# Second chunk of v loaded earlier and transposed by DMA instead of by TensorE, in a fused attention and gated-FFN kernel

## Chip, cores, metric

One core of one Trainium2 chip. The metric is the device time of one execution in microseconds (us), median of several runs. Lower is better.

## The reference

```python
qn = q / (norm(q, axis=1) + 1e-06)          # q, k, v: [4, 6016, 256] float32
kn = k / (norm(k, axis=1) + 1e-06)
a  = softmax(kn.transpose(0, 2, 1) @ qn / tau)       # [4, 256, 256]
x  = (v @ a).reshape(24064, 256)
gate = sigmoid(x @ w_gate); val = x @ w_val          # d_ff 1536
out  = (gate * val) @ w_out
```

## The kernel before

The kernel folds the softmaxed 256 x 256 matrix into the weights (G = a @ w_gate, H = a @ w_val), so the FFN reads v itself. It works through four batches of v in chunks of 512 rows, 12 chunks a batch. A chunk has 12 steps of 128 FFN columns, each with two matmuls for `ps_gate`, two for `ps_val`, a sigmoid on ScalarE and a product on VectorE. The output matmuls of a chunk run in the steps of the next one.

The FFN needs v transposed. For all chunks but the first two this is a transposing DMA on SP's queue. All loads but two (the first chunk of q and of k, at the very start) convert float32 to bf16 and go through GpSimd's queue.

```python
    def transpose_v(b, ci, ps=None, late=None):
        t0, nt = groups[ci]
        v_sb = vs.pop((b, ci))
        vT = vtpool.tile([P, TPC * CB, P], BF16, tag="vT", name="vT")
        flat = v_sb[:, :nt, :].rearrange("p t c -> p (t c)")
        if ps is None:
            nc.sync.dma_start_transpose(out=vT[:, : nt * CB, :], in_=flat)
        else:
            for n in range(nt * CB):
                nc.tensor.transpose(out=ps[:, n, :], in_=flat[:, ds(n * P, P)], identity=ident_bf)
            half = nt * CB // 2
            nc.vector.tensor_copy(out=vT[:, :half, :], in_=ps[:, :half, :])
            (nc.scalar.copy if late is None else late)(vT[:, half : nt * CB, :], ps[:, half : nt * CB, :])
        ...
    # loads, after q and k of batch 0 and chunk 0 of v
    for fg in range(NFG):                       # three groups of 512 columns
        for w, src in enumerate((moe_w_gate, moe_w_val)):
            nc.gpsimd.dma_start(out=w_sb[w][fg], in_=...)
    load_v(0, 1)
    nc.gpsimd.dma_start(out=w_out_sb, in_=...)
    ...
    # side work of batch b, by slot = chunk * 12 + step
            if (nb, nci) == (0, 1):
                at(7, lambda: transpose_v(0, 1, psm.tile(...)))      # TensorE
            elif nb < B:
                at(ci * FC + 2, transpose_v, nb, nci)                # DMA
            if lb < B:
                at(ci * FC + 0, load_v, lb, lci)
        ...
            at(max(0, s0 - 20), load_qk, n, t0, nt)                  # next batch
```

A slot only fixes the order of instructions within each queue. GpSimd and SP run ahead of TensorE as far as their own waits let them.

## Time and profile before

| | before |
|---|---|
| time, median of the 3 first runs | 831.2 us (830.94 to 831.29) |
| span of the profiled run | 829.0 us |
| TensorE busy | 816.1 us, 98% of the span |
| TensorE idle after 37 us | one wait of 0.36 us, at 51.95 |
| DMA engines | 9 tenths busy or more up to some 80 us, less after |

The lines that carry this are in the prediction. In a timeline row, the first two numbers are start and length, and the bracket at the end tells how long the engine sat idle before it and what released it. TensorE is the bound, so only what TensorE does or waits for counts.

### The profile page before, as it was taken

How to read it: one execution, taken by the hardware profiler on the slowest of the kernel's cores; microseconds unless marked ns; L12 is line 12 of the kernel's file. 1: busy time of each engine (PE TensorE's matmuls, PEld its weight loads, DVE VectorE, ACT ScalarE, POOL GpSimd, SP SyncE). 2: the span in 40 equal slices, each digit the busy share in tenths (PEclk: the TensorE clock that was granted, in tenths of full speed). 3: DMA queues.
4: the chain of work that ended last, by engine and by line, in shares of the span. 5: the costliest groups of instructions: out<-in, count | busy, mean ns of one | idle time of the engine just before them, and what ended most of it. 6: DMA issues, size and time to landing. Idle time of an engine off the chain costs nothing.

```text
span 829.0 us, 13765 instructions
## 1 busy us (share of the span) xinstructions
PE 816.1 (98%) x5192; PEld 502.6 (61%) x5206; DVE 588.9 (71%) x1022; ACT 391.6 (47%) x644; POOL 83.1 (10%) x159
## 2 busy tenths in 40 slices
PE   7899999999999999999999999999999999999998
PEld 4556666665665666665575666666566566666666
DVE  6577777887667777778767777777766666666664
ACT  4654444446644444445654444444655444444442
POOL 5531100002120100000211010000000000000000
PEclk9999999999999999999999999999999999999999
DMA  9999623226946433223875352223323423322111
GB/s 209 207 206 207 113 52 86 57 60 131 159 87 124 96 85 60 57 52 84 156 140 126 81 105 59 51 63 75 64 62 63 72 52 87 67 48 73 43 36 71
DMA packets 78739, 77.17 MB, mean 93 GB/s; under 512 B 50769, under 2 KB 55633, under 8 KB 78673
## 3 DMA queue, kind: packets, MB, share of 16 engines
q0 software_dynamic: 23920, 38.81, 28.3%
q1 hardware_dynamic: 54608, 36.97, 17.6%
q8 instruction: 40, 0.66, 0.3%
q10 hardware_dynamic: 144, 0.52, 0.2%
q14 instruction: 27, 0.21, 0.1%
HBM read 78.64 MB, written 24.64 MB: 125 GB/s over the span
## 4 chain that ended last, share of the span: by engine, by line
PE 94%; DMA 4%; DVE 1%; issue 0%; POOL 0%; ACT 0%; POOLq 0%; ACTq 0%
PE ps_o L88 30%; PE ps_gate L88 29%; PE ps_val L88 29%; PE ps_s L88 4%; DMA q_sb<-in_q_dram 3%; PE ps_gh L88 2%; DMA w_val<-in_moe_w_val_dram 1%; DVE hT L423 0%; ACT g_sb L422 0%; DVE sq L176 0%; PE ps_n L88 0%; POOL k_sb L97 0%; POOL q_sb L97 0%; PE ps_tp L393 0%; DVE out_sb L449 0%
## 5 line engine op out<-in xcount | busy, mean ns | idle before, releaser
L423 DVE TENSOR_TENSOR hT<-ps_val,g_sb 128x512 bf16<-128x512 f32 (+1 forms) x576 | 391.2, 680 | 206.3 <-ACT g_sb L422 201.9
L422 ACT ACTIVATE g_sb<-ps_gate 128x512 bf16<-128x512 f32 (+1 forms) x576 | 338.1, 588 | 386.0 <-PE ps_gate L88 380.0
L88 PE MATMUL ps_gate<-vT,gh_G 128*128 128x512 bf16 (+1 forms) x1152 | 337.6, 375 | 0.6 <-ACT g_sb L422 0.4
L88 PE MATMUL ps_val<-vT,gh_H 128*128 128x512 bf16 (+1 forms) x1152 | 337.4, 375 | 0.4
L88 PE MATMUL ps_o<-w_out_sb,hT 128*128 128x256 bf16 x2256 | 326.2, 273 | 0.0
L88 PEld LDWEIGHTS <-hT 128*128 128x128 bf16 x2256 | 220.7, 98 | 124.8
L88 PEld LDWEIGHTS <-gh_H 128*128 128x128 bf16 x1152 | 112.7, 98 | 131.6 <-issue 1.4
L88 PEld LDWEIGHTS <-gh_G 128*128 128x128 bf16 x1152 | 112.4, 98 | 38.5 <-issue 0.6
L106 POOL DMA_DIRECT2D v_sb<-in_v_dram x48 | 25.6, 533 | 619.9 <-DMA vT<-v_sb 485.8
L449 DVE COPY out_sb<-ps_o 128x256 f32<-128x256 f32 x188 | 77.9, 414 | 13.5 <-PE ps_o L88 13.5
L88 PE MATMUL ps_s<-k_sb,q_sb 128*128 128x256 bf16 x376 | 66.0, 272 | 5.7 <-DMA k_sb<-in_k_dram 4.3
L88 PEld LDWEIGHTS <-q_sb 128*128 128x128 bf16 x376 | 36.6, 98 | 14.1 <-issue 6.3
L215 DVE TENSOR_TENSOR acc<-acc,sq 128x1024 bf16<-128x1024 bf16 (+1 forms) x66 | 44.2, 669 | 0.0
L176 DVE TENSOR_TENSOR sq<-q_sb 128x1024 bf16<-128x1024 bf16 (+2 forms) x44 | 29.4, 668 | 2.7 <-DMA q_sb<-in_q_dram 2.7
L97 POOL DMA_DIRECT2D k_sb<-in_k_dram x48 | 26.3, 549 | 16.5 <-DMA k_sb<-in_k_dram 8.9
L97 POOL DMA_DIRECT2D q_sb<-in_q_dram x48 | 26.2, 545 | 16.0 <-DMA q_sb<-in_q_dram 8.6
L176 DVE TENSOR_TENSOR sq<-k_sb 128x1024 bf16<-128x1024 bf16 (+2 forms) x34 | 22.4, 658 | 0.9 <-ACT sq L174 0.9
L376 ACT ACTIVATE gh_G<-ps_gh,rrow 128x512 bf16<-128x512 f32 x21 | 14.4, 687 | 12.7 <-PE ps_gh L88 8.8
L174 ACT ACTIVATE sq<-k_sb 128x1024 bf16<-128x1024 bf16 (+1 forms) x11 | 11.2, 1018 | 14.6 <-DMA k_sb<-in_k_dram 11.8
L88 PE MATMUL ps_busy<-ones_wide,ones_bf 128*128 128x512 bf16 x57 | 16.3, 412 | 1.7 <-DVE shift L127 1.6
L378 DVE TENSOR_SCALAR gh_H<-ps_gh,rrow 128x512 bf16<-128x512 f32 x22 | 16.4, 743 | 1.6 <-PE ps_gh L88 1.6
L472 DVE TENSOR_TENSOR acc<-acc,sq 128x1024 bf16<-128x1024 bf16 x16 | 11.1, 692 | 5.1 <-ACT sq L174 4.8
(65 smaller groups left out, 124.5 us busy)
## 6 DMA issues: line engine op xcount, KB each, us to landing
out_dram<-out_sb SPq DMA_DIRECT2D x44, 512.0 KB, 2.9
v_sb<-in_v_dram POOLq DMA_DIRECT2D x44, 256.0 KB, 3.8
q_sb<-in_q_dram POOLq DMA_DIRECT2D x43, 256.0 KB, 7.8
k_sb<-in_k_dram POOLq DMA_DIRECT2D x43, 256.0 KB, 8.5
out_dram<-out_sb SPq DMA_DIRECT2D x4, 384.0 KB, 2.5
w_gate<-in_moe_w_gate_dram POOLq DMA_DIRECT2D x3, 256.0 KB, 6.8
w_val<-in_moe_w_val_dram POOLq DMA_DIRECT2D x3, 256.0 KB, 7.4
w_out_sb<-in_moe_w_out_dram POOLq DMA_DIRECT2D x1, 768.0 KB, 12.6
```

Source lines behind the costliest of these rows:

```text
L88: nc.tensor.matmul(out, lhsT=lhsT, rhs=rhs, start=start, stop=stop, **kw)
L97: nc.gpsimd.dma_start(out=tl[:, :nt, :], in_=rows(src, b)[:, t0 : t0 + nt, :])
L106: nc.gpsimd.dma_start(out=v_sb[:, :nt, :], in_=rows(v, b)[:, t0 : t0 + nt, :])
L174: nc.scalar.activation(out=sq[:, :nt, :], in_=src[:, :nt, :], func=ACT.Square)
L176: engine.tensor_tensor(out=sq[:, :nt, :], in0=src[:, :nt, :], in1=src[:, :nt, :], op=ALU.mult)
L215: nc.vector.tensor_tensor(out=acc[:, :nt, :], in0=acc[:, :nt, :], in1=st[b]["sq", w][:, :nt, :], op=ALU.add)
L376: nc.scalar.activation(out=dst, in_=ps, func=ACT.Copy, scale=r)
L378: nc.vector.tensor_scalar(out=dst, in0=ps, scalar1=r, scalar2=None, op0=ALU.mult)
L422: nc.scalar.activation(out=g_sb[:, :n], in_=ps_gate[:, :n], func=ACT.Sigmoid)
L423: nc.vector.tensor_tensor(out=hts[b, ci][:, f, :n], in0=ps_val[:, :n], in1=g_sb[:, :n], op=ALU.mult)
L449: nc.vector.tensor_copy(out=out_sb[:, s, :], in_=ps)
L472: nc.vector.tensor_tensor(out=acc[w], in0=acc[w], in1=sq[w], op=ALU.add)
```

## The change

It takes TensorE's eight transposes and the two copies that follow them out of the first chunk. So that the transposing DMA which replaces them can start in time, v's second chunk is loaded one place earlier.

```diff
     for fg in range(NFG):
+        if fg == NFG - 1:
+            load_v(0, 1)
         for w, src in enumerate((moe_w_gate, moe_w_val)):
             nc.gpsimd.dma_start(...)
-    load_v(0, 1)
     nc.gpsimd.dma_start(out=w_out_sb, ...)
@@
-            if (nb, nci) == (0, 1):
-                at(7, lambda: transpose_v(0, 1, psm.tile(...)))
-            elif nb < B:
-                at(ci * FC + 2, transpose_v, nb, nci)
+            if nb < B:
+                at(ci * FC + (0 if (b, ci) == (0, 0) else 2), transpose_v, nb, nci)
```

More of the change, by code (lines that the diff above doesn't have):

```diff
@@ L526, in side_work @@
             lb, lci = (b, ci + 2) if ci + 2 < NCH else (b + 1, ci + 2 - NCH)
-            if (nb, nci) == (0, 1):
-                at(7, lambda: transpose_v(0, 1, psm.tile([P, TPC * CB, P], BF16, tag="m", name="ps_tp")))
-            elif nb < B:
-                at(ci * FC + 2, transpose_v, nb, nci)
+            if nb < B:
+                at(ci * FC + (0 if (b, ci) == (0, 0) else 2), transpose_v, nb, nci)
             if lb < B:
```

## The prediction

> **What bounds the kernel now.** I read the page's first part and its chain first, then TensorE's timeline around the one spot that the diff touches, then the same stretch of the chain, then the tile of the transposed v, and last the DMA queues in three windows.
>
> The page:
>
> ```profile
> PE 816.1 (98%) x5192; PEld 502.6 (61%) x5206; DVE 588.9 (71%) x1022; ACT 391.6 (47%) x644; POOL 83.1 (10%) x159
> ...
> PE 94%; DMA 4%; DVE 1%; issue 0%; POOL 0%; ACT 0%; POOLq 0%; ACTq 0%
> ```
>
> TensorE is busy for 98% of the span and is 94% of the chain that ended last. From 37 us, when the first weight matrix lands, the chain is nearly all matmuls in program order. So whatever leaves TensorE's order, or whatever gap closes in it, moves the end by as much, and a new gap does the opposite.
>
> TensorE's timeline, 47.95 to 53.97 us (start, length, engine, operation, count, idle before). The removed work lies here: v's second chunk goes through TensorE at step 7 of 12 of the first chunk.
>
> ```profile
> 48.39 0.59 PE L88 MATMUL ps_gate<-vT,gh_G 128*128 128x512 bf16 x2
> 48.82 0.59 PE L88 MATMUL ps_val<-vT,gh_H 128*128 128x512 bf16 x2
> 49.25 0.61 PE L393 MATMUL ps_tp<-ident_bf,v_sb 128*128 128x128 bf16 x8
> 49.70 0.59 PE L88 MATMUL ps_gate<-vT,gh_G 128*128 128x512 bf16 x2
> ...
> 50.56 0.59 PE L88 MATMUL ps_gate<-vT,gh_G 128*128 128x512 bf16 x2
> ...
> 51.95 0.59 PE L88 MATMUL ps_gate<-vT,gh_G 128*128 128x512 bf16 x2 [0.36 <-ACT g_sb L422]
> 52.67 0.59 PE L88 MATMUL ps_val<-vT,gh_H 128*128 128x512 bf16 x2
> 53.10 0.59 PE L88 MATMUL ps_gate<-vT,gh_G 128*128 128x512 bf16 x2
> ...
> 53.97 0.59 PE L88 MATMUL ps_gate<-vT,gh_G 128*128 128x512 bf16 x2
> ```
>
> A step without extras takes 0.86 us (49.70 to 50.56). The step with the transposes takes 1.31 (48.39 to 49.70), two later ones 1.39 and 1.15. The row at 53.97 is the first matmul of chunk 1, the first reader of the tile that the change makes differently.
>
> The chain of waits over the same stretch says why two later steps are long:
>
> ```profile
> 50.72 0.45 PE ps_gate L88 x2
> ...
> 51.30 0.61 ACT g_sb L422
> ...
> 51.93 0.70 DVE hT L423
> ...
> 52.67 0.59 PE ps_val L88 x2
> ```
>
> ScalarE copied half of the transposed tile at 50.81 for 0.59 us, after VectorE had copied the other half. That pushed its next sigmoid to 51.30, VectorE's product to 51.93, and TensorE's next ps_val, which waits for that PSUM buffer, to 52.67.
>
> The transposed tile (first window 48 to 50 us, second 124 to 126): its DMA form lands very differently in the two.
>
> ```profile
> L390 SPq DMA_TRANSPOSE vT<-v_sb x1: 1337/1337/1337, 49.0 to 49.0; - x1
> ...
> DMA to landing us min/median/max: 16.2/16.2/16.2
> ```
>
> ```profile
> DMA to landing us min/median/max: 3.7/3.7/3.7
> ```
>
> The DMA queues while the 16.2 us one moved its data (52.8 to 64.5 us):
>
> ```profile
> q0 software_dynamic: 1083, 1.99, 94.8%
> q1 hardware_dynamic: 1054, 0.26, 17.8%
> ```
>
> and while the output weights came in (42.8 to 46.4 us):
>
> ```profile
> q0 software_dynamic: 1356, 0.72, 144.6%
> ```
>
> The loads (q0) leave no room: the page's DMA row is at 9 tenths for the first tenth of the span. The transpose (q1) moves 256 KB in about 1,024 packets of 256 B and gets just about one packet for each of q0's.
>
> **What the Trainium skill says.** "DMA: Bandwidth & Descriptors", section "Queues, rings and completion order": an engine takes turns between the queues it has work for, one packet each. The trace agrees: 1,083 packets of q0 beside 1,054 of q1. "Advanced Engine Details and Errata", section "X-Bar Transpose (TRN2)": "TRN2 transpose DMAs are as fast as regular DMAs". In the quiet part this holds (3.7 us, against the 3.8 us of the page's median v load of as many bytes); in the saturated part it doesn't, 16.2 us against 12.6 for the v load just before it. "TensorE: Matmul & The Clock Gate", section "Part 4: PE-mode transpose": the result goes to PSUM and has to be copied out, some 275 ns for one in a kernel. The copies are what cost here; the matmul record is 219 ns, and eight pipelined ones advance TensorE by 0.45 us.
>
> **The change part by part.**
>
> 1. Removed from TensorE: eight transposes, 49.25 to 49.70, 0.45 us.
> 2. Removed from ScalarE and VectorE: copies of 0.59 and 0.41 us. On TensorE they cost the two long steps: 1.39 - 0.86 = 0.53, and 1.15 - 0.86 = 0.29. Without them each step gives ScalarE 0.59 and VectorE 0.68 us of work in 0.86, so I expect no wait to replace them. Sum of 1 and 2: about 1.25 us. Check: 48.39 to 53.97 is 5.58 us for five steps; five at 0.865 are 4.33. Chunk 1 could start at 52.7.
> 3. Moved: the load of chunk 1 of v takes the place of the third gate weights in q0. They landed at 41.2 us (issued 33.18, 8.0 later), the value weights at 42.5 (33.87 + 8.6), v at 43.7 (34.58 + 9.1). All are 256 KB, 1.26 us each at the 208 GB/s of this stretch. So v lands at about 41.1 and the weights at 42.4 and 43.7. TensorE reads these first at 44.07 and 45.37, so both keep about 1.6 us. No cost.
> 4. Added: one DMA transpose on SP. The program puts it in step 0, but SP waits only for v and has nothing ahead of it: issue at about 41.15. The existing one, issued at 48.97, showed its first packet at 52.85, 3.9 us later; in the quiet part it was 1.7. If the extra 2.2 us is a fixed number of q0's packets ahead of it, the smaller packets here (1 KB, then 512 B, where the other had 2 KB) halve it: first packet between 43.8 and 45.0.
>    Then the sharing. While the other transpose ran, q0 moved 1.99 MB in 11.7 us, 170 GB/s; without it q0 moves 208. It lost 0.45 MB, 2.1 us of its time, so one transpose packet takes 2.1 x 16 / 1,054 = 32 ns of an engine. It got 88 packets per us (1,024 in the 11.65 us from first to last). The output weights alone: 1,356 packets in 3.6 us, 377 per us, 42 ns a packet on each engine, and they would end at about 46.6. Beside such small ones a pair takes 42 + 32 = 74 ns, so 216 pairs per us.
>    Start at 43.8: all 1,024 run beside the output weights in 4.7 us and end at 48.5. The other one landed 0.7 us after its last packet, so this one at 49.2. Start at 45.0: 377 x 1.6 = 603 pairs in 2.8 us, the other 421 beside 2 KB loads at 88 per us in 4.8, end 52.6, landed at 53.3. Needed at 52.7. By the same sum the break-even start is 44.8.
> 5. Given back by the queue: q0 loses 2.1 us to the new transpose. The output weights land at 49.8 instead of 47.7 (issued 35.11, 12.6 to landing), needed at 54.83 - 1.25 = 53.6. The next batch's first k (issued 39.11, 12.3) lands at 53.5, needed at 57.87 - 1.25 = 56.6. Chunk 2 of v lands near 51.0 instead of 48.9; its transpose then lands at 51.0 + 16.2 = 67.2, needed at 70.88 - 1.25 = 69.6. In time, by 2.4 us where it was 5.7.
>
> Sum: -1.25 us if the transpose is in time: 831.2 - 1.25 = 829.95, call it 830.0.
>
> **The rivals.**
>
> A. The transpose comes late and TensorE waits at the start of chunk 1, a new gap in place of the old ones. For: 16.2 us for its sibling, taken over whole, would land at 57.4; the gap is 4.7 us and the time 831.2 + 3.4 = 834.6. Against: small packets on the other queue through most of it. The late case of step 4, landing at 53.3, waits 0.6 and leaves -0.65: 830.5.
>
> B. The gain stays but the second transpose, now pushed back, is late for chunk 2. For: margin shrinks, and a first packet held up behind the first transpose, then still under way, would shrink it more. Each us late costs one: perhaps 831 to 832.
>
> C. The ScalarE and VectorE copies were hiding another wait, so only the 0.45 us comes back: 830.7. Against: both engines have slack of 0.18 us or more in a plain step.
>
> D. Late weights. It needs over 1.6 us of error in a landing; 832 at most.
>
> **Range and chances.** I give about 60% to on time (829.8 to 830.2), 25% to a partly filled gap or C (830.3 to 831.2), 15% to A or B beyond break-even, up to 834.6. Predicted 830.2 us, 8 in 10 within 829.6 to 832.4. A change of 2% is 16.6 us, and nothing here reaches a third of that either way: faster 0.5%, same 99%, slower 0.5%.
>
> **What would show it right or wrong.** Right: no ps_tp rows after 37 us; steps 7 to 11 of chunk 0 at 0.86 us each; chunk 1's first ps_gate near 52.7 with no idle before it; the new transpose issued near 41.1 and landed before 52.7, so in under 11.6 us; the weights of the third group in before 44.1 and 45.4; the second transpose landed before 69.6. Wrong: an idle of TensorE before chunk 1's first ps_gate released by the DMA of the transposed tile (A), the same at chunk 2 (B), waits on g_sb left in steps 9 to 11 (C), or on w_gate or w_val in steps 3 and 4 (D). A first packet later than 44.8, or a transpose packet dearer than 32 ns, is the likeliest error.

## The result

| | before | changed |
|---|---|---|
| time, median of 6 runs | 831.21 us (830.94 to 831.69) | 834.25 us (832.10 to 836.04) |
| span of the profiled run | 829.0 | 833.3 |

The ratio is 1.0035, 95% interval 1.0018 to 1.0051. Ratios here are the mean time of one kernel's runs over that of the other's in the same rounds, so not quite the ratio of the medians. The changed kernel is slower by 3 us, and its runs spread over 4 us where those of before spread over 0.75.

The page of the changed kernel, its engine line and its chain:

```profile
PE 816.1 (98%) x5184; PEld 502.0 (60%) x5198; DVE 588.5 (71%) x1021; ACT 391.2 (47%) x643; POOL 83.4 (10%) x159
...
PE 90%; DMA 8%; DVE 1%; POOL 0%; issue 0%; ACT 0%; POOLq 0%
```

The eight matmuls are gone from TensorE (5,184 for 5,192), and the DMA's share of the chain went from 4% to 8%. That share alone decides nothing: the last but two of the runs below (`e11_hold_lead8`), as fast as the kernel before, has 8% too. TensorE's timeline of the changed kernel:

```profile
49.37 0.59 PE L88 MATMUL ps_gate<-vT,gh_G 128*128 128x512 bf16 x2
...
51.97 0.59 PE L88 MATMUL ps_gate<-vT,gh_G 128*128 128x512 bf16 x2
...
55.27 0.60 PE L88 MATMUL ps_gate<-vT,gh_G 128*128 128x512 bf16 x2 [2.27 <-DMA vT<-v_sb]
...
91.86 0.61 PE L88 MATMUL ps_gate<-vT,gh_G 128*128 128x512 bf16 x2 [2.38 <-DMA vT<-v_sb]
```

49.37 to 51.97 is three steps of 0.87 us: the steps are as short as forecast. Then TensorE waits twice on the transposed tile: at 55.27 for chunk 1, whose transpose the change added, and at 91.86 for chunk 3, whose transpose was there before and was in time then.

The sum closes: TensorE's first step of chunk 1 could have begun at 51.97 + 0.87 = 52.84 and began at 55.27, where the kernel before began it at 53.97, so +1.30. From the first to the second store of results the delay against before grows from 1.31 to 3.86 us, so chunk 3 adds 2.55. The two stores in SP's timeline, changed:

```profile
74.50 0.34 SPq L452 DMA_DIRECT2D out_dram<-out_sb  x1
...
94.18 0.33 SPq L452 DMA_DIRECT2D out_dram<-out_sb  x1
```

and before:

```profile
73.19 0.35 SPq L451 DMA_DIRECT2D out_dram<-out_sb  x1
...
90.32 0.34 SPq L451 DMA_DIRECT2D out_dram<-out_sb  x1
```

The delay then stays at 3.8 to 3.9 up to the last stores, and about 0.5 us more lies after them: 4.3, the difference of the two spans.

How long the transposes took. First the tile's landing times in the changed kernel, chunk 1's and chunk 3's, then chunk 3's in the kernel before:

```profile
DMA to landing us min/median/max: 13.9/13.9/13.9
...
DMA to landing us min/median/max: 16.8/16.8/16.8
```

```profile
DMA to landing us min/median/max: 10.6/10.6/10.6
```

The queues of the changed kernel, from the issue of chunk 1's transpose to its first packet (41.3 to 45.3 us), while it ran (45.3 to 54.7), and while chunk 3's ran (79.9 to 91.3):

```profile
q0 software_dynamic: 1350, 0.80, 138.7%
...
q0 software_dynamic: 1134, 1.49, 94.8%
q1 hardware_dynamic: 1053, 0.26, 25.3%
...
q0 software_dynamic: 707, 1.27, 67.3%
q1 hardware_dynamic: 1081, 0.33, 21.2%
```

and of the kernel before while chunk 3's ran (79.3 to 83.9):

```profile
q1 hardware_dynamic: 1055, 0.26, 64.2%
q0 software_dynamic: 233, 0.41, 48.5%
```

For 4 us after its issue chunk 1's transpose moves nothing, then it shares packet for packet with the loads (1,134 beside 1,053) for 9.4 us. Chunk 3's transpose met 233 packets of loads in the kernel before and meets 707 in the changed one.

Why it meets more, from GpSimd's timeline. GpSimd's transfers wait for one another: in these rows none is issued before the one eight places ahead of it has landed (48.02 after the output weights at 47.7, and 52.84 after 52.5 in the changed kernel). The load of chunk 3 of v stands eight places behind the output weights. Before:

```profile
48.02 0.53 POOL L106 DMA_DIRECT2D v_sb<-in_v_dram  x1 [3.27 <-DMA w_out_sb<-in_moe_w_out_dram]
...
71.65 0.53 POOL L97 DMA_DIRECT2D k_sb<-in_k_dram  x1 [0.70 <-DMA k_sb<-in_k_dram]
84.82 0.53 POOL L106 DMA_DIRECT2D v_sb<-in_v_dram  x1 [12.64 <-DMA vT<-v_sb]
```

Changed:

```profile
52.84 0.53 POOL L106 DMA_DIRECT2D v_sb<-in_v_dram  x1 [7.99 <-DMA w_out_sb<-in_moe_w_out_dram]
...
78.13 0.53 POOL L97 DMA_DIRECT2D k_sb<-in_k_dram  x1 [0.72 <-ACT g_sb L423]
92.34 0.53 POOL L106 DMA_DIRECT2D v_sb<-in_v_dram  x1 [13.68 <-DMA vT<-v_sb]
```

The output weights, slowed by the transpose beside them, landed 17.3 us after issue instead of 12.6. GpSimd therefore waited 7.99 us where it had waited 3.27, and the last load it could issue before it had to wait for chunk 3's transpose moved from 71.65 to 78.13. Of these 6.5 us, 4.8 come from that wait; the rest from a second one of the same kind, 4.25 us at 68.43, for a load of q that was issued at 54.56 and landed after 13.3 us, with chunk 2's transpose beside it. Chunk 3's transpose was issued at 74.97 (before at 73.66), into loads still under way.

### The profile page after: what moved, and what is told of

It reads as the page before. It is cut to its first block, busy times and chain, and to the rows that moved or that the text cites. A ratio compares the mean times of both kernels' runs of the same rounds, so it can differ in the third digit from the quotient of the medians.

```text
span 833.3 us, 13748 instructions
## 1 busy us (share of the span) xinstructions
PE 816.1 (98%) x5184; PEld 502.0 (60%) x5198; DVE 588.5 (71%) x1021; ACT 391.2 (47%) x643; POOL 83.4 (10%) x159
## 4 chain that ended last, share of the span: by engine, by line
PE 90%; DMA 8%; DVE 1%; POOL 0%; issue 0%; ACT 0%; POOLq 0%
PE ps_o L88 29%; PE ps_gate L88 28%; PE ps_val L88 28%; DMA vT<-v_sb 4%; PE ps_s L88 3%; DMA k_sb<-in_k_dram 3%; PE ps_gh L88 2%; DMA v_sb<-in_v_dram 1%; DVE hT L424 0%; DVE sq L177 0%; ACT g_sb L423 0%; PE ps_n L88 0%; POOL q_sb L97 0%; POOL w_val L141 0%; POOL w_gate L141 0%
## 6 DMA issues: line engine op xcount, KB each, us to landing
w_out_sb<-in_moe_w_out_dram POOLq DMA_DIRECT2D x1, 768.0 KB, 17.3
```

## The experiments

The theory to test: the gain is real; the transposing DMA is late because it shares the engines with the loads; and it also pushes the loads back, so that a later transpose is late as well. The first rival is that the new order of loads is the harm. A second is that the transposing DMA is slow by itself at this place. A third, for the wait at chunk 3, is that SP's queue or the added transpose causes it directly. An edit is shown against the changed kernel, that of `e5_pe_step3` against the kernel before with the loads in the new order, that of `e6_wout_twice` against the kernel before. The four runs up to the first hold had a kernel before with a median of 831.25 us beside them, the next four 830.98, the last three 831.16.

### The order of loads alone (e1_order_only)

```diff
+            if (nb, nci) == (0, 1):
+                at(7, lambda: transpose_v(0, 1, psm.tile(...)))    # TensorE, as before
-            if nb < B:
-                at(ci * FC + (0 if (b, ci) == (0, 0) else 2), transpose_v, nb, nci)
+            elif nb < B:
+                at(ci * FC + 2, transpose_v, nb, nci)
```

> The load of v's second chunk stays ahead of the third weights, but TensorE transposes it at step 7 as before. My theory (the transposing DMA is late, because it shares the engines with the loads, and it pushes the loads): the order of loads alone costs nothing, since the weights still land over 1 us before their use: 831.2 us within 0.3, no wait of TensorE for a DMA after 37 us. Rival (the later weights or the earlier v are themselves the loss): over 832.

Measured: 831.10 us (830.97 to 831.13), ratio 0.9995 (0.998 to 1.001). No wait of TensorE for a DMA after 37 us. The order of loads costs nothing, and the first rival falls.

### The DMA transpose alone (e2_dma_only)

```diff
-        if fg == NFG - 1:
-            load_v(0, 1)
         ...
+    load_v(0, 1)
     nc.gpsimd.dma_start(out=w_out_sb, ...)
```

> The other half alone: transposed by DMA, but loaded behind the third weights as before. v lands at 43.7 instead of 41.3, first transpose packet at about 47.8 (4.1 us after issue), when most of the output weights' small packets are gone, so nearly all of it runs beside 2 KB packets: about 11.7 us more, landed near 60. My theory: TensorE waits 7 us at chunk 1 and the time is 835 to 838 us. Rival (the load order causes the waits): no worse than the changed kernel's 834.3.

Measured: 839.24 us (838.35 to 839.72), ratio 1.0091 (1.0074 to 1.0108). More than my 835 to 838. Timeline, and TensorE's busy time and granted clock from 60 to 64 us (window, length, then busy time and count for each engine, then clock, DMA share, GB/s):

```profile
59.22 1.03 PE L88 MATMUL ps_gate<-vT,gh_G 128*128 128x512 bf16 x2 [6.28 <-DMA vT<-v_sb]
60.05 1.06 PE L88 MATMUL ps_val<-vT,gh_H 128*128 128x512 bf16 x2
```

```profile
60.00:64.00 4.00, 4.00 (x14) 1.92 (x13) 0.92 (x2) 1.19 (x2) 1.42 (x3) 0.50 1.13 205
```

The transpose was issued at 43.74 and landed 15.4 us later; the wait is 6.28 us. What I had left out: after it TensorE ran at half its clock (0.50) and a pair of matmuls took 1.03 to 1.06 us for 0.59, for some 5 us. Half of that is lost too: -1.25 + 6.28 + about 2.6 is 7.6, and the results come 7.87 us later. The output weights, with most of their packets ahead of the transpose, landed after 12.6 us as before, and there was no wait at chunk 3. So the earlier load helps, but by too little.

### No transpose of chunk 1 at all (e3_skip)

```diff
+            if (nb, nci) == (0, 1):
+                at(0, lambda: vts.__setitem__((0, 1), vts[0, 0]))   # wrong data on purpose
```

> Wrong result on purpose: chunk 1 reads the transposed tile of chunk 0, so chunk 1 of v is loaded but not transposed by anybody. It measures the gain alone. My theory: 1.25 us less than before, 830.0 us within 0.2, steps 7 to 11 of chunk 0 at 0.86 us each, and no second wait at chunk 3, for the loads are not pushed. Rival (the copies on ScalarE and VectorE hid another wait): 830.7. Rival (the wait at chunk 3 is due to the order of loads): it is still there and the time is over 832.

Measured: 829.87 us (829.69 to 829.94), ratio 0.998 (0.9965 to 0.9995), wrong result as meant. 1.38 us less than before, for 1.25 forecast, and TensorE never waits on a transposed tile. By the first stores of the two traces the gain is 1.10 us. The gain of the removed work is real and whole, so all the loss of the changed kernel, 834.25 - 829.87 = 4.4 us, belongs to the added DMA.

### Loads held until the transpose has landed (e4_hold)

```diff
+    def hold():
+        nc.gpsimd.tensor_copy(out=held_sb, in_=vts[0, 1][:, 0, 0, 0:1])
 ...
+            if (b, ci) == (0, 0):
+                at(0, hold)          # ahead of load_v(0, 2) and the next batch's q and k
```

> The changed kernel, with one thing added: GpSimd copies one column of the transposed tile before it issues chunk 2 of v and the next batch's q and k, so these loads cannot start before the transpose has landed, and it has the DMA engines to itself once the output weights are in. My theory (sharing is what makes it late): first packet still near 45.4, but landed near 49 to 50 instead of 55.2, no wait of TensorE at chunk 1, the loads about 2 us behind those of the kernel before, so a small wait at chunk 3 or none: 830.0 to 831.5 us. Rival (the transposing DMA is slow by itself here, whatever else runs): landed at 53 or later, 831.5 us or more.

Measured: 835.38 us (833.41 to 836.50), ratio 1.0044 (1.0028 to 1.006). The time is not what I expected, but the traces tell the two halves apart:

```profile
50.53 0.19 POOL L405 COPY held_sb<-vT 128x1 bf16<-128x1 bf16 x1 [14.43 <-DMA vT<-v_sb]
```

```profile
71.21 0.60 PE L88 MATMUL ps_gate<-vT,gh_G 128*128 128x512 bf16 x2 [0.72 <-DMA vT<-v_sb]
...
91.45 1.04 PE L88 MATMUL ps_gate<-vT,gh_G 128*128 128x512 bf16 x2 [2.94 <-DMA vT<-v_sb]
```

Chunk 1's transpose, issued at 41.45, landed after 9.0 us instead of 13.9 and TensorE doesn't wait at chunk 1. So it is late because of the sharing, not by itself. (One 0.38 us wait on the second value weights at 40.60 is in this run too; these stand ahead of the hold in GpSimd's queue.) But the held loads are pushed back as the theory has it, and the waits come back at chunks 2 and 3. After the 2.94 us the clock halves again, as the first of these windows shows; the second is the changed kernel, at full clock after its wait of 2.38:

```profile
92.00:94.00 2.00, 2.00 (x9) 0.92 (x8) 0.56 (x1) 0.60 (x1) 2.00 (x4) 0.50 0.46 26
```

```profile
92.00:94.00 2.00, 2.00 (x13) 1.17 (x12) 0.87 (x2) 0.60 (x1) 1.66 (x4) 1.00 0.29 16
```

### TensorE's transposes at another step (e5_pe_step3)

```diff
-                at(7, lambda: transpose_v(0, 1, psm.tile(...)))
+                at(3, lambda: transpose_v(0, 1, psm.tile(...)))    # load order as changed
```

> No DMA transpose for chunk 1: the load order of the changed kernel, and TensorE transposes chunk 1 of v at step 3 instead of step 7. v has landed by 41.3 us, step 3 is at about 44. Steps 1 to 6 take 1.3 us on TensorE, with 0.25 us or more of slack on ScalarE and VectorE each, so their two copies should delay nothing. My theory (of the 1.4 us that the transposes cost, only 0.45 is TensorE's own work and the rest is copies in the way of short steps): 830.4 us within 0.3. Rival (the copies delay TensorE wherever they stand): 831.1, as before.

Measured: 830.65 us (830.20 to 830.75), ratio 0.9993 (0.998 to 1.0005): not clear of the kernel before. In the trace the stores come 0.37 us earlier than before, where 0.8 was hoped for. The rest went into two late ps_val at steps 6 and 8 (0.13 and 0.15 us) and into 0.14 us by which the run with the new order of loads alone stores later than before, too (73.33 for 73.19). So the copies hurt less in the long steps, not nothing.

### Three holds (e7_hold3)

The hold is repeated after the transposes of chunks 2 and 3 (`if b == 0 and ci < 3: at(..., hold, nci)`).

> As the run with the hold, but GpSimd waits three times, for the transposed tiles of chunks 1, 2 and 3, before it issues more loads, so that each of the three transposing DMAs soon has the engines to itself. My theory (the waits at chunks 2 and 3 come from loads that run beside the transposes): no wait of TensorE on a transposed tile, 830.0 us within 0.4. Rival (the loads of the next batch then come too late, or the transposes are slow by themselves): 831.5 or more.

Measured: 834.22 us (831.75 to 835.08), ratio 1.0036 (1.0023 to 1.005). I expected 830.0 and was wrong, again for the reason of the theory. The profiled run (831.75) shows chunk 3's transpose landing 4.8 us after issue for 16.8, no wait at chunks 1 to 3, and the wait moved to chunk 4, the first without a hold, where the transpose took 16.0 us:

```profile
105.69 0.60 PE L88 MATMUL ps_gate<-vT,gh_G 128*128 128x512 bf16 x2 [1.58 <-DMA vT<-v_sb]
```

The four slower runs (833.08 to 835.08) have no trace. Each run's mean granted clock: 1.000 for the profiled one, 0.999 for 833.08 and 0.997 for the other three, so what they lost is not shown, but a halved clock for a few us fits three of them.

### Loads asked for later (e8_lead8)

```diff
-            at(max(0, s0 - 20), load_qk, n, t0, nt)
+            at(max(0, s0 - 8), load_qk, n, t0, nt)
```

> The changed kernel with the next batch's q and k asked for 8 steps ahead of their use instead of 20, so two pairs fewer (four loads of 1.26 us) stand in GpSimd's queue ahead of the v load that waits for chunk 3's transpose. My theory (the wait at chunk 3 comes from loads pushed back into the time of chunk 3's transpose): the wait at chunk 1 stays, 2.3 us or so, the one at chunk 3 goes: 832.3 us within 0.7. Rival (chunk 3's transpose is late for another reason, such as the order of SP's queue): both waits stay, 834.3.

Measured: 834.09 us (832.88 to 834.38), ratio 1.0032 (1.0019 to 1.0046). The trace is that of the run of 832.88: one wait of 2.52 us at chunk 1, none at chunk 3, whose transpose landed 13.9 us after issue, at 88.9, for a first use at 89.37. With four loads fewer ahead of it, chunk 3 is in time, if only by some 0.4 us, though SP's queue is the same: the third rival falls in its first form. The median misses my range by 1 us. The profile doesn't show those slower runs. Their mean granted clock: 0.997 for 834.38 and 834.20, 0.999 for 833.98, and 1.000 for the profiled run. Over 832 us a mean of 0.997 is some 2.5 us of full clock lost (an estimate from these numbers), so a halved clock fits two of the three; which wait did it is open.

### The changed kernel again (e9_again)

Unaltered.

> The changed kernel unaltered, for the spread of its runs (832.1 to 836.0). My theory: the two waits vary by some tenths of a us to 2 us from run to run, and where one passes about 2.5 us TensorE's granted clock falls to half for some us after it, as in the two runs where the waits were 2.9 and 6.3 us; below that it stays at full. So median near 834 with a similar spread, and this profile shows half speed after a wait of TensorE if and only if that wait is over 2.5 us.

Measured: 835.39 us (832.03 to 837.66), ratio 1.0047 (1.0025 to 1.007). The profiled run was the slowest, 837.66. Its waits are 2.16 us at chunk 1 and 3.42 at chunk 3:

```profile
92.66 1.03 PE L88 MATMUL ps_gate<-vT,gh_G 128*128 128x512 bf16 x2 [3.42 <-DMA vT<-v_sb]
```

```profile
93.00:95.00 2.00, 2.00 (x8) 0.92 (x7) 0.34 (x1) 0.60 (x1) 1.85 (x4) 0.50 0.65 97
```

Over all profiles, waits of 0.46 to 2.52 us left the clock at full and those of 2.94, 3.42 and 6.28 halved it. The Trainium skill, "TensorE: Matmul & The Clock Gate", section "Part 1: The HAM clock gate (the "warmup" mystery)", has the clock fall to half after an idle window of about 3.4 us, in windows that run freely. The runs agree in kind; 2.94 us was enough here. The half clock lasted 3.4 us in two runs (91.4 to 94.8 with the first hold, 92.2 to 95.7 here) and 6.8 in the third (57.7 to 64.6 with the DMA transpose alone), once and twice that window. In the first two it began 0.1 and 0.4 us before the wait was over. So where in a window a wait falls may matter as much as its length: that was not tested, and the runs give no threshold. The clock explains a part of the spread: the two profiled runs of the changed kernel differ by 1 us at chunk 3's wait and by a stretch at half clock after it.

### One hold and the shorter lead together (e11_hold_lead8)

The edits of the first hold and of the shorter lead.

> One hold (for chunk 1) and q and k asked for 8 steps ahead instead of 20. The hold alone took away the wait at chunk 1 and left 0.7 us at chunk 2 and 2.9 at chunk 3; the shorter lead alone took away the wait at chunk 3. My theory: only the wait of some 0.7 us at chunk 2 stays, 830.7 us within 0.5. Rival (the two do not add up, a wait over 2.5 us stays somewhere): 832.5 or more.

Measured: 831.14 us (830.51 to 831.75), ratio 0.9994 (0.9982 to 1.0007). One wait is left, 0.56 us at chunk 2; the two cures add up. In time the same as before.

### Loads pushed without the change (e6_wout_twice)

```diff
-    nc.gpsimd.dma_start(out=w_out_sb, ...)
+    for tl in (w_out_sb, w_out_two):      # on the kernel before; w_out_two is read by nobody
+        nc.gpsimd.dma_start(out=tl, ...)
```

> The kernel before (chunk 1 transposed by TensorE at step 7), with the output weights loaded a second time into a tile that nobody reads, so all later loads come about 4 us later, as they did in the changed kernel (output weights landed 4.8 us later there). No early DMA transpose is in it. My theory (pushing the loads is by itself enough to make chunk 3's transpose late): chunk 3's transpose, landed at 84.3 before, lands at 88 to 91, TensorE needs it at 88.1, so a wait of 0 to 3 us at chunk 3: 831.3 to 835. Rival (chunk 3's wait comes from the added transpose itself): landed before 86, 831.1.

Measured: 831.58 us (831.57 to 831.67), ratio 1.000 (0.9985 to 1.0016). Too small to show in the time, but plain in the trace: chunk 3's transpose took 14.9 us for 10.6, landed at 88.5, and TensorE waits there, with chunk 1 still transposed by TensorE:

```profile
88.59 0.61 PE L88 MATMUL ps_gate<-vT,gh_G 128*128 128x512 bf16 x2 [0.46 <-DMA vT<-v_sb]
```

Pushing the loads by some 4 us is by itself enough to make chunk 3's transpose late, so the added transpose is not needed for it, which was the third rival's second form. The push was smaller than in the changed kernel (last load before the wait at 75.47, there at 78.13, before at 71.65), and so was the wait; that it accounts for the whole 2.4 us is not shown.

### Every transpose of the first batch with a hold (e10_hold9)

As with three holds, for chunks 1 to 9 (`ci < 9`).

> As the run with three holds, with nine: GpSimd waits for each transposed tile of the first batch up to chunk 9 before it issues more loads. In the run with three, the wait moved on to chunk 4 (1.6 us), the first without a hold. My theory (each transpose that meets a queue of loads is late, and a held queue only moves the meeting on): with all of them held no wait of TensorE on a transposed tile is left, 829.9 us within 0.3, spread as small as that of the kernel before. Rival (the held loads come too late for the scores of the next batch, or a wait turns up elsewhere): 831.0 or more.

Measured: 830.26 us (830.14 to 830.86), correct, ratio 0.9986 (0.9974 to 0.9999) against before. TensorE waits on no transposed tile; the stores come 1.05 us earlier than before. The transposes of chunks 3 and 4 land after 4.7 and 3.6 us. The median is 0.06 above my range, and the spread is back to 0.7 us. This version beats both kernels, by 0.9 us (only just clear of the noise) and by some 4.

## Why the prediction was wrong

What held:

- **Steps 1 and 2, the gain.** 1.25 us forecast, 1.38 measured with the transpose taken away, 0.87 us a step.
- **Step 3, the order of loads.** Free, as said.
- **The arrival of v and the issue of the transpose.** 41.15 forecast, 41.28 measured.
- **The sharing packet for packet**, and its price for the loads: 1.49 MB in 9.4 us is 158 GB/s, 50 less than 208, 2.3 us of loading lost for 2.1 forecast.
- **The class:** within 2%.

What failed are steps 4 and 5. Step 4 had the transpose start early enough to run mostly beside the output weights and land between 49.2 and 53.3; it started later, met 2 KB loads with more than half of its packets, and landed at 55.2, so TensorE waited 2.27 us at chunk 1. Step 5 had the pushed loads harm nothing after it; they made chunk 3's transpose late, so TensorE waited 2.38 us there.

- **Step 4, the first packet.** I let the delay of 3.9 us between issue and first packet shrink with the size of the loads' packets, to 2.65 at best, and made "break-even start 44.8" the hinge, a later one the likeliest error. It was 4.0 us (41.28 to 45.31), beside packets of 1 KB and 512 B. The idea that a fixed number of packets stands ahead has fallen: the delay was 3.9 beside 2 KB packets and no shorter beside small ones (4.0 in the run with the DMA transpose alone, too). The loads moved 0.80 MB meanwhile in either kernel (1,350 packets here, 441 before, from 48.97 to 52.84), so equal bytes would fit as well as equal time. What sets it is open. At a start of 45.31 my own sum gives the last packet at 53.7 (486 packets by 47.6, the other 538 at 88 per us in 6.1); it came at 54.6, and landed at 55.2 against the 52.8 needed. So 0.5 us of lateness at the start turned into most of a 2.4 us wait. From 48 to 50 us the loads and the transpose together moved only 162 GB/s, which the sum had not either. I cannot show why.
- **Step 5, the loads.** I followed the pushed loads to chunk 2 and stopped there. Chunk 2 was in time, but only because TensorE was late by then: its tile landed at 69.9, not 67.2, past the 69.6 that I gave as the limit, and was first read at 72.19. And the output weights landed at 52.5, not 49.8: beside the transpose the loads went at 187 packets per us (504 from 45.3 to 48 us), where the output weights alone had gone at 377. I had spread the loss evenly over the queue. GpSimd's wait for them, eight places on, carried the delay to chunk 3, which rival B had not named. With the further wait at 68.43 that makes the second wait of TensorE, 2.4 to 3.4 us, about half of the loss.
- **Rival A** gave 834.6 for the case of a 16.2 us transpose, close to the 834.25 measured, by coincidence: it was for one wait of 4.7 us that never was; it was two of about 2.3. I gave it and B 15% together.
- **The clock.** No line of the prediction asked what a wait does to TensorE's clock. In the three runs with a wait of 2.94 us or more it halved, and such a run pays for the wait more than once.

## What to carry to other kernels

Here a transposing DMA of many small packets was cheap on idle engines (3.7 us to landing in the median) and slow among loads (13.9 us for chunk 1, 16.2 for chunk 2 before the change), so before moving a transpose off the bounding engine, look at how busy the DMA engines are at that moment and what the same transfer took there already. When a transfer is added to a full queue, follow the pushed loads as far as the queue runs ahead, not just to their next reader. Holding back loads that nobody needs yet can be worth more than starting a transfer early.

## What the Trainium skill lacked or had wrong

- "Advanced Engine Details and Errata", section "X-Bar Transpose (TRN2)": that transposing DMAs are as fast as regular ones agrees with the trace on idle engines (3.7 us to landing in the median, and 3.8 for a load of v). The page says nothing of a transpose beside loads: there the same 256 KB took 13.9 us for chunk 1, 16.2 for chunk 2 before the change, and 20.8 where chunk 2's stood behind chunk 1's in the queue (the DMA transpose alone). Loads of 256 KB issued in the same stretch took 10.3 to 17.1 us, so this is not shown to be slower than a regular DMA.
- "DMA: Bandwidth & Descriptors", section "Latency and other measured facts": it gives some 600 ns to the first byte on this path, and not from where it counts. From the start of SP's instruction, which itself takes some 1.4 us, to the first packet of a transpose the runs show 1.7 us in the quiet part and 3.8 to 4.0 for chunks 1 and 2 among loads. For chunk 3, behind a store of results in the same queue, it was 4.9 in the changed kernel and 5.6 before.
- The same page, section "Queues, rings and completion order": the turns by packet agree with the trace, but it doesn't draw the consequence: a queue of 256 B packets takes a turn for every packet of the other, and the output weights, in 512 B packets, landed after 17.3 us instead of 12.6.
- "TensorE: Matmul & The Clock Gate", section "Part 1: The HAM clock gate (the "warmup" mystery)": about 3.4 us of idle time for the half clock; here a wait of 2.94 us did it and one of 2.52 didn't. The length of the half clock (3.4, 3.4 and 6.8 us) agrees with its window.
